# Two copies to the upper partitions: transfers issued by GpSimd in place of ScalarE calls, in a convolution and GELU kernel on one core

## The chip, the cores and the metric

The kernel runs on one core of a Trainium2 chip. The metric is the device time of one execution in microseconds; the time before is the median of three runs. Engines are named as the profile names them: PE (TensorE), with its weight loads as PEld, DVE (VectorE), ACT (ScalarE), POOL (GpSimd) and SP, which only issues transfers.

## The reference

A causal depthwise convolution of seven taps, its weights softmaxed for each of eight heads, feeds a two-layer network with an exact GELU and no biases. Cut to what matters:

```python
# x: (8, 4096, 192), weight: (8, 7), moe_w_in: (192, 2048), moe_w_out: (2048, 192), all float32
w = softmax(weight, axis=-1)                       # one set of 7 taps for each head of 24 channels
conv[b, s, h, g] = sum_k w[h, k] * x_pad[b, s + k, h, g]     # 6 rows of zeros ahead of each sequence
h = conv.reshape(32768, 192) @ moe_w_in
out = (0.5 * h * (1 + erf(h / sqrt(2)))) @ moe_w_out
```

## The kernel before, in words

**Blocks.** The 32768 rows are two halves of 16384. A block takes the same stretch of both halves, one on partitions 0 to 63 (LO), the other on 64 to 127 (UP). There are 35 blocks: six of 256 rows a half, then 29 of 512. For each block DVE transposes the input (`t`, line 968) and computes the taps (calls 1 to 6, lines 338 and 343; the last writes `xc`). The first tap (`f`, line 1107) is computed by ACT; in blocks 13, 18, 23 and 28 two thirds of it are left to DVE as call `0`. PE multiplies by `w_in` (line 1242) in 16 slices into two PSUM buffers `hp`, ACT applies the GELU to each slice (line 1149) into `gT`, and PE multiplies by `w_out` in the next block's time, interleaved with that block's first product. A slice's product has to wait until the GELU two slices earlier has emptied its buffer.

**Two forms of the second product.** In N blocks it is computed directly (line 1327): 48 rounds of four 64x64 matmuls side by side, beside 48 of the first product. The 17 blocks of the list `ST` are S blocks (9, 10, 12, 14, 15, 17, 19, 20, 22, 24, 25, 27, 29 to 33). There a Strassen-like scheme (line 1376) saves PE four rounds, 92 in place of 96 in the block that follows, at the cost of sums on other engines. Ahead of the products DVE, or POOL by accumulating transfers, forms sums of parts of `gT`: `S1`, `S3`, `Dn`, `S4` (lines 662 to 699; `cp` is the plain copy of 512 KB, line 673, ahead of an accumulated `Dn`). Behind them partial products in four PSUM banks X, D, Y and V are joined:

- ACT (`st_copy`, line 740): `p15` copies X to an SBUF tile `gs`; `e` copies a piece of V into D; `p3` copies X's upper half to `tqs`; `u` copies X's lower half to `uu[LO]`. Then `-g` writes -U to `gs[UP]`, and `-u` writes -U to `uu[UP]`, both read from `uu[LO]`.
- DVE (`st_post`): `k0` (line 746) takes `gs` from Y's upper half, `k4` (line 754) adds Y to `gs`, `k3` (line 750) adds `uu` to `tqs`. Then `ev.0`, `ev.1`, `ev.2` (lines 461 and 766) transpose the results into `osb`, from which SP stores them.

`gs` and `tqs` have two buffers each, `uu` one. A bank that a block gives back is taken by a later one: `k4` frees Y, and if the next block is an S block too it takes that bank as its V. PE writes V some 8 us after the start of the block in which that product runs.

**The order** of the work is written out. `LIST` gives DVE's order by block (it runs ahead of PE by up to a block), `SLOT` says before which of a block's 16 GELUs ACT does what (`2:u.9` in list 11: `u` of block 9 ahead of GELU 2 of block 11), and `GLIST` is the order of POOL's queue: transfers, and the six columns that a block's convolution takes over from the block before (`halo`). Every engine works its queue strictly in order, so an instruction that waits holds all behind it. In the text below S + 8 means 8 us after the first `w_in` matmul of the block in which PE is.

Of the kernel before, what the change touches and what calls it, by code (L numbers as in the profile page):

```python
# [11 lines left out]
def bass_lightweight_conv__then__act_gelu_exact_kernel(  # L12
# [63 lines left out]
        9: "t10 ev.0.6 ev.2.6 1 ev.1.6 2 3 4 5 6",  # L76
        10: "t11 ev.0.7 1 2 3 4 ev.1.7 ev.2.7 5 6",
        11: "t12 1 2 3 S1.0.9 4 5 S1.1.9 ev.0.8 ev.1.8 S1.2.9 6",
        12: "Dn.1.9 ev.2.8 S3.2.9 1 S4.0.9 2 S4.1.9 k0.0.9 3 S1.0.10 4 5 S1.1.10 ev.2.9 t13 S1.2.10 Dn.0.10 6",
        13: "S3.2.10 k4.0.9 Dn.1.10 S4.0.10 S4.1.10 t14 k0.0.10 0 ev.0.9 1 2 ev.2.10 k3.0.9 3 ev.1.9 4 5 6",  # L80
        14: "t15 1 2 3 S1.0.12 ev.0.11 4 5 k4.0.10 k3.0.10 S1.1.12 S1.2.12 ev.1.11 ev.1.10 Dn.1.12 ev.2.11 S3.2.12 6",
        15: "S4.0.12 t16 S4.1.12 ev.0.10 k0.0.12 1 2 3 ev.2.12 4 5 6",
        16: "1 t17 2 3 S1.0.14 k3.0.12 4 ev.1.12 ev.0.13 k4.0.12 5 S1.1.14 ev.0.12 ev.2.13 S1.2.14 ev.1.13 Dn.1.14 6",
        17: "S3.2.14 S4.0.14 t18 S4.1.14 1 k0.0.14 S1.0.15 2 3 4 S1.1.15 ev.2.14 Dn.0.15 S1.2.15 5 S3.2.15 6",
        18: "k4.0.14 S4.0.15 Dn.1.15 S4.1.15 k0.0.15 0 ev.0.14 1 2 3 k3.0.14 ev.1.14 ev.2.15 t19 4 5 k4.0.15 6",
        19: "t20 ev.0.15 S1.0.17 1 2 ev.0.16 3 k3.0.15 S1.1.17 4 S1.2.17 ev.1.16 S3.2.17 5 ev.2.16 S4.0.17 Dn.1.17 S4.1.17 ev.1.15 6",
        20: "k0.0.17 t21 1 2 3 ev.2.17 4 5 6",
# [12 lines left out]
        33: "k0.0.30 t34 1 2 S1.0.31 k3.0.29 S1.1.31 Dn.0.31 ev.2.30 ev.1.29 S1.2.31 S4.0.31 3 S3.2.31 4 k4.0.30 ev.0.29 Dn.1.31 S4.1.31 k0.0.31 5 6",  # L100
        34: "k3.0.30 S1.0.32 1 ev.2.31 ev.1.30 Dn.0.32 S1.1.32 S1.2.32 S3.2.32 2 3 k4.0.31 ev.0.30 S4.0.32 Dn.1.32 S4.1.32 ev.0.31 k0.0.32 4 5 S1.0.33 6",
        35: "ev.2.32 S1.1.33 S1.2.33 k3.0.31 S3.2.33 ev.1.31 Dn.0.33 Dn.1.33 k4.0.32 ev.0.32 S4.0.33 k0.0.33 S4.1.33 k3.0.32 ev.1.32 ev.2.33 k4.0.33 ev.0.33 k3.0.33 ev.1.33",
# [3 lines left out]
        8: "0:f0.10 4:f1.10 6:f2.10",  # L106
        9: "1:f0.11 2:f1.11 5:f2.11 8:f0.12 8:f1.12",
        10: "0:f2.12 7:p15.9 13:e.9",
        11: "0:p3.9 2:u.9 4:-g.9 6:p15.10 8:f2.13 10:f0.14 11:-u.9 13:e.10 15:f1.14",
        12: "1:p3.10 2:u.10 4:f2.14 5:-g.10 8:-u.10 11:f0.15 13:f1.15",  # L110
        13: "0:f2.15 7:p15.12 10:f0.16 11:f1.16 13:e.12",
        14: "0:f2.16 2:u.12 3:-g.12 4:p3.12 8:-u.12 9:f0.17 10:f1.17",
        15: "5:f2.17 7:p15.14 8:f2.18 13:e.14",
        16: "0:p3.14 2:u.14 4:-g.14 6:p15.15 11:-u.14 13:e.15",
        17: "0:u.15 2:p3.15 4:-g.15 5:f0.19 6:f1.19 8:f2.19 11:f0.20 12:-u.15",
        18: "4:f1.20 7:p15.17 8:f2.20 11:f0.21 13:e.17 15:f1.21",
        19: "1:p3.17 3:f2.21 4:u.17 7:-g.17 8:f0.22 9:-u.17 12:f1.22",
        20: "0:f2.22 7:p15.19 12:f2.23 13:e.19",
        21: "0:p3.19 2:u.19 4:-g.19 6:p15.20 9:-u.19 13:e.20",
        22: "1:p3.20 2:u.20 4:f0.24 5:-g.20 6:f1.24 8:f2.24 9:-u.20 12:f0.25",  # L120
        23: "5:f1.25 7:p15.22 9:f2.25 11:f0.26 13:e.22",
        24: "0:f1.26 2:p3.22 3:u.22 4:f2.26 7:-g.22 8:f0.27 9:f1.27 11:-u.22 12:f2.27",
        25: "6:p15.24 13:e.24",
        26: "0:p3.24 2:u.24 4:-g.24 6:p15.25 8:-u.24 10:f2.28 12:f0.29 13:e.25",
        27: "1:p3.25 2:u.25 3:-g.25 5:f1.29 6:f2.29 9:f0.30 12:-u.25",
        28: "2:f1.30 4:f2.30 7:p15.27 10:f0.31 10:f1.31 13:e.27",
        29: "0:p3.27 2:f2.31 4:u.27 7:-g.27 9:-u.27 12:f0.32",
        30: "0:f1.32 2:f2.32 7:p15.29 9:f0.33 10:f1.33 12:f2.33 14:e.29",
        31: "0:p3.29 2:u.29 4:-g.29 6:p15.30 8:-u.29 10:f0.34 10:f1.34 13:f2.34 14:e.30",
# [60 lines left out]
    with es:  # L190
# [27 lines left out]
        tq = sbt("tq", [128, TB], F32)  # L218
        hp = [pst("hp%d" % i, [128, 2 * TB]) for i in range(2)]
# [37 lines left out]
        S_UH = sem("S_UH")  # L257
        S_ST = sem("S_ST")
# [3 lines left out]
        S_AD = {k: sem("S_AD" + k) for k in ("S3.0", "S3.1", "S3.2", "Dn.0", "Dn.1", "cp.0", "cp.1")}  # L262
# [447 lines left out]
        def st_copy(a, m, name):  # L710
# [6 lines left out]
            if name[0] != "-":  # L717
                st_done(a, m, {"p15": max("P1", "P5", key=FORM[m][1].get), "e": "Ea", "p3": "P3", "u": "P6"}[name])
            if name == "e":
                dst, src = bank(BK[m]["D"], UP, HA), bank(BK[m]["V"], LO, HA)  # L720
            else:
                dst, src = {
                    "p15": (gs(m)[:, :], bank(BK[m]["X"])),
                    "u": (uu[LO, :], xb(LO)),
                    "-u": (uu[UP, :], uu[LO, :]),
                    "p3": (tqs(m)[LO, :], xb(UP)),
                    "-g": (gs(m)[UP, :], uu[LO, :]),
                }[name]
            if name[0] == "-":
                a.wait_ge(S_AC, ac(m, "u"))  # L730
# [3 lines left out]
            if name == "-g":  # L734
                a.wait_ge(S_DP, dp(m, "k0"))
# [4 lines left out]
            a.activation(out=dst, in_=src, func=AF.Copy, scale=-1.0 if name[0] == "-" else 1.0).then_inc(S_AC)  # L740

        def st_post(v, m, name):
            if name == "k0":
                st_done(v, m, "P7")
                v.wait_ge(S_AC, ac(m, "p15"))
                ins = v.tensor_tensor(tqs(m)[UP, :], bank(BK[m]["Y"], UP), gs(m)[UP, :], ALU.subtract)
            elif name == "k3":
                v.wait_ge(S_AC, max(ac(m, "-u"), ac(m, "p3")))
                v.wait_ge(S_DP, dp(m, "k0"))
                ins = v.tensor_tensor(tqs(m)[:, :], tqs(m)[:, :], uu[:, :], ALU.add)  # L750
            else:
                v.wait_ge(S_MM2, MMC[m + 1])
                v.wait_ge(S_AC, ac(m, "-g"))
                ins = v.tensor_tensor(gs(m)[:, :], bank(BK[m]["Y"]), gs(m)[:, :], ALU.add)
# [25 lines left out]
        def store(e, m):  # L780
# [714 lines left out]
```

## Time and profile before

| | |
|---|---|
| median of 3 runs | 667.44 us (666.6 to 667.59) |
| profiled execution | 668.08 us, of which the span from first to last instruction is 666.1 us |
| granted TensorE clock | 1.000 |
| busy, share of the span | PE 99%, PEld 68%, DVE 92%, ACT 91%, POOL 13% |
| GELU calls, line 1149 | 510 of 1.023 us |
| `-u`, line 740, uu from uu | 17 of 0.629 us |
| `-g`, line 740, gsm or p5s from uu | 17 of 0.63 us |
| `u`, line 740, uu from ob | 17 of 0.582 us |
| first taps of 512 columns, line 1107 | 73 of 0.718 us |
| tap of 1536 elements, line 343 | 145 of 1.807 us |
| `k0`, `k4`, `k3` | 0.695, 0.68 and 0.68 us |

A row of the profile names line, engine, operation and what is written from what; buffer numbers are left out. A `busy` PE is not a PE at its peak, since matmuls are pipelined and their ends are modelled; so the prediction reads PE's progress from the times at which its blocks start. "Idle before" is an engine's idle time just ahead of an instruction, with what ended it.

### The profile page before, as it was taken

Reading aid. Unit: us, or ns where it says so; the run is one execution under the profiler, and the core shown is the slowest. Engines: PE = TensorE matmul, PEld = TensorE weight load, DVE = VectorE, ACT = ScalarE, POOL = GpSimd, SP = SyncE. Lnnn points to the kernel's source line nnn. Section 1 sums busy time; section 2 is a strip of 40 time slices with the busy share of each in tenths; the row PEclk is TensorE's granted clock in tenths of the full one; section 3 lists DMA queues with packets and bytes.
Section 4 is the critical chain, followed back from the end, with each engine's and each line's share of the span. In section 5 each row is a group of like instructions: output and inputs, shape, how many; then the busy total and the mean of one; then the engine's idle time right before and its main releaser. Section 6 shows DMA issues by size and latency. Waiting matters only on the chain.

```text
span 666.1 us, 27899 instructions
## 1 busy us (share of the span) xinstructions
PE 660.9 (99%) x12776; PEld 450.1 (68%) x12776; DVE 615.3 (92%) x550; ACT 608.7 (91%) x723; POOL 86.1 (13%) x137
## 2 busy tenths in 40 slices
PE   8999999999999999999999999999999999999998
PEld 8999655557755657655757665756665766777678
DVE  5889998999999989999999999999999999999962
ACT  8899988888999998999998999998999999999994
POOL 8000540020002020002020101010101010111000
PEclk9999999999999999999999999999999999999999
DMA  9745674566044859144849145849245558223345
GB/s 154 158 99 135 108 122 97 101 146 140 18 116 94 186 125 218 19 96 113 190 101 224 31 96 123 182 97 208 51 96 113 143 121 185 50 50 81 76 95 136
DMA packets 144422, 78.14 MB, mean 117 GB/s; under 512 B 129329, under 2 KB 137585, under 8 KB 144305
## 3 DMA queue, kind: packets, MB, share of 16 engines
q1 hardware_dynamic: 129328, 49.42, 33.2%
q0 software_dynamic: 13856, 26.36, 20.0%
q8 instruction: 100, 1.64, 1.1%
q10 hardware_dynamic: 1120, 0.59, 0.3%
q14 instruction: 18, 0.14, 0.1%
HBM read 31.51 MB, written 25.17 MB: 85 GB/s over the span
## 4 chain that ended last, share of the span: by engine, by line
PE 96%; DMA 2%; DVE 1%; POOL 1%; issue 0%; ACT 0%; DVEq 0%; POOLq 0%
PE hp L1242 49%; PE ob L1376 24%; PE ob L1327 17%; PE ob L1282 4%; DMA xin<-in_x_dram 1%; PE ob L1432 1%; PE hp L1432 1%; DVE acc L343 1%; DMA win<-in_moe_w_in_dram 1%; POOL win L825 0%; DVE xT L968 0%; POOL xTb L358 0%; DVE xc L343 0%; DVE acc L338 0%; POOL wout L857 0%
## 5 line engine op out<-in xcount | busy, mean ns | idle before, releaser
L1149 ACT ACTIVATE gT<-hp 128x1024 bf16<-128x1024 f32 x510 | 512.0, 1023 | 45.6 <-PE hp L1242 39.2
L1242 PE MATMUL hp<-xc,win 64*64 64x512 bf16 (+2 forms) x6036 | 426.3, 366 | 0.7 <-DVE xc L343 0.5
L343 DVE SCALAR_TENSOR_TENSOR acc<-xT,wcol,acc 128x1536 f32<-128x1536 f32 (+1 forms) x165 | 282.3, 1711 | 7.3 <-ACT acc L1107 4.1
L1242 PEld LDWEIGHTS hp<-xc,win 64*64 64x64 bf16 (+1 forms) x6036 | 212.4, 105 | 105.7 <-ACT gT L1149 13.4
L1376 PE MATMUL ob<-gT,wot 64*64 64x512 bf16 x1088 | 206.5, 376 | 0.0
L1376 PE MATMUL ob<-gT,wst 64*64 64x512 bf16 (+2 forms) x1088 | 191.2, 323 | 0.0
L1327 PE MATMUL ob<-gT,wot 64*64 64x512 bf16 x2112 | 144.8, 376 | 0.0
L1376 PE MATMUL ob<-s_S,wot 64*64 64x384 bf16 (+2 forms) x816 | 125.6, 305 | 0.0
L1376 PEld LDWEIGHTS ob<-gT,wst 64*64 64x64 bf16 x1088 | 93.3, 107 | 13.7
L1327 PEld LDWEIGHTS ob<-gT,wot 64*64 64x64 bf16 x2112 | 64.4, 107 | 49.6
L1376 PEld LDWEIGHTS ob<-gT,wot 64*64 64x64 bf16 x1088 | 83.2, 107 | 18.4 <-DVE osb L766 0.5
L1376 PE MATMUL ob<-s_S,wst 64*64 64x512 bf16 x272 | 75.1, 376 | 0.0
L1376 PE MATMUL ob<-s_Dn,wst 64*64 64x512 bf16 x272 | 75.0, 376 | 0.0
L1376 PEld LDWEIGHTS ob<-s_S,wot 64*64 64x64 bf16 x816 | 64.3, 107 | 15.3
L968 DVE STREAM_TRANSPOSE xT<-xin 128x1536 f32<-128x1536 f32 (+2 forms) x39 | 59.3, 1530 | 4.6 <-DMA xin<-in_x_dram 3.7
L343 DVE SCALAR_TENSOR_TENSOR xc<-xT,wcol,acc 128x1536 bf16<-128x1536 f32 (+1 forms) x33 | 56.6, 1716 | 1.1 <-PE hp L1242 0.5
L662 POOL DMA_DIRECT2D gT<-gT x34 | 29.5, 866 | 211.0 <-DVE s_S L690 211.0
L1107 ACT ACTIVATE acc<-xT,wcol 128x512 f32<-128x512 f32 (+1 forms) x79 | 55.1, 701 | 0.0
L690 DVE TENSOR_TENSOR s_S<-gT 128x1024 bf16<-128x1024 bf16 (+1 forms) x51 | 43.5, 855 | 3.0 <-ACT gT L1149 2.8
L1282 PE MATMUL ob<-wout,gT 64*128 64x192 bf16 x768 | 42.1, 243 | 0.5 <-issue 0.5
L699 DVE TENSOR_TENSOR s_S<-gT,s_Dn 128x2048 bf16<-128x2048 bf16 x34 | 40.9, 1211 | 0.7
L1282 PEld LDWEIGHTS ob<-wout,gT 64*128 64x128 bf16 x768 | 35.1, 94 | 4.0 <-issue 0.7
(90 smaller groups left out, 388.1 us busy)
## 6 DMA issues: line engine op xcount, KB each, us to landing
out_dram<-osb SPq DMA_DIRECT2D x124, 192.0 KB, 3.6
xin<-in_x_dram SPq DMA_DIRECT2D x116, 192.0 KB, 4.2
gT<-gT POOLq DMA_DIRECT2D x17, 512.0 KB, 5.0
s_Dn<-gT POOLq DMA_DIRECT2D x9, 512.0 KB, 2.9
s_Dn<-s_S POOLq DMA_DIRECT2D x9, 512.0 KB, 6.5
gT<-gT POOLq DMA_DIRECT2D x17, 256.0 KB, 3.8
xin<-in_x_dram SPq DMA_DIRECT2D x18, 96.0 KB, 2.7
win<-in_moe_w_in_dram POOLq DMA_DIRECT2D x24, 64.0 KB, 3.5
```

Of the source, the lines that this page charges most:

```text
L343: return e.scalar_tensor_tensor(dst, src, wk, a, op0=ALU.mult, op1=ALU.add)
L662: e.dma_start(quad(m, 1, 0, k, k1 - k), quad(m, 0, 0, k, k1 - k), accum_op=ALU.add).then_inc(S_AD["S3.%d" % q], 16)
L690: ins = v.tensor_tensor(t("S1"), quad(m, 1, 0, k, n), quad(m, 1, 1, k, n), ALU.add)
L699: ins = v.tensor_tensor(t("S4"), quad(m, 0, 1, k, n), t("Dn"), ALU.add)
L968: v.transpose(out, src).then_inc(S_TR)
L1107: a.activation(out=acc[n % 2][:, p * TB : p * TB + w], in_=ap(xT[n % 2], p * XW + HX, [[NP * XW, 128], [1, w]]), func=AF.Copy, scale=wcol[ ...
L1149: a.activation(out=ap(gT[n % 2], (i % 2 * NF + i // 2) * TB if n in ST else i * c * 2 * w, dst), in_=ap(ob, 2 * TB, [[4 * TB, 128], *src[1 ...
L1242: ins = t.matmul(hbuf(u, slice(fo, fo + fw), o, w), ap(win, f1, [[NP * F, 64], [2, fw]]), xc[n % 2][r, p * TB : p * TB + w], start=(p == 0 ...
L1282: ins = t.matmul(bb[sub], gT[m % 2][r, c0 : c0 + 128], wout[r, CH[sub][i] * C : (CH[sub][i] + 1) * C], start=(ph == 0 and k == 0), stop=(p ...
L1327: ins = t.matmul(bank(BK[m][j], slice(64 * h, 64 * h + 64), w), ap(wot, 64 * hf * NF * C + CH[h][i] * C + 64 * j, [[NF * C, 64], [1, 64]]) ...
L1376: ins = t.matmul(bank(BK[m][bk], slice(64 * cg, 64 * cg + 64))[:, c0 : c0 + w], wt_, x, start=(e == mine[0]), stop=(e == mine[-1] or e in ...
L1432: ins = t.matmul(banks(m, g)[h], gT[m % 2][:, c0 : c0 + 128], wout[:, CH[h][i] * C : (CH[h][i] + 1) * C], start=(i == 0), stop=(i == NF - 1),)
```

## The change

`-g` and `-u` are no ScalarE calls any more. POOL issues two transfers in their place, `cg` (`uu[LO]` to `gs[UP]`) and `cu` (`uu[LO]` to `uu[UP]`), 64 rows of 512 float32 each. A transfer can't negate, so the signs go elsewhere: `p15` copies X with scale -1, `k0` adds, `k4` subtracts, and `k3` multiplies `uu` by a column `sgn` (1 on the lower, -1 on the upper partitions, set by two memsets on DVE at the start) before it adds. `k4` waits for `cg`, `k3` for `cu`, `cg` for `u` and `k0`, and the next S block's `u` for the `cg` before it. `LIST`, `SLOT` and `GLIST` are new for blocks 8 to 35; they hold the same calls but for the replaced ones, in another order. The parts of the lists that the prediction speaks of are kept here.

```diff
 LIST
-        12: "Dn.1.9 ev.2.8 S3.2.9 1 S4.0.9 2 S4.1.9 k0.0.9 3 S1.0.10 4 5 S1.1.10 ev.2.9 t13 S1.2.10 Dn.0.10 6",
-        18: "k4.0.14 S4.0.15 Dn.1.15 S4.1.15 k0.0.15 0 ev.0.14 1 2 3 k3.0.14 ev.1.14 ev.2.15 t19 4 5 k4.0.15 6",
-        20: "k0.0.17 t21 1 2 3 ev.2.17 4 5 6",
-        34: "k3.0.30 S1.0.32 1 ev.2.31 ev.1.30 Dn.0.32 S1.1.32 S1.2.32 S3.2.32 2 3 k4.0.31 ev.0.30 S4.0.32 Dn.1.32 S4.1.32 ev.0.31 k0.0.32 4 5 S1.0.33 6",
+        12: "ev.1.8 S1.2.9 S3.2.9 ev.2.8 1 Dn.1.9 t13 S4.0.9 k0.0.9 S4.1.9 S1.0.10 2 3 4 ev.2.9 5 S1.1.10 S1.2.10 Dn.0.10 S3.2.10 Dn.1.10 6",
+        18: "0 k4.0.14 Dn.1.15 S4.0.15 k3.0.14 S4.1.15 k0.0.15 1 t19 ev.1.14 2 ev.0.14 ev.2.15 3 4 5 6",
+        20: "ev.0.15 S4.0.17 k0.0.17 S4.1.17 1 t21 2 3 ev.2.17 4 5 6",
+        34: "ev.0.30 S1.0.32 S1.1.32 1 k3.0.30 ev.2.31 Dn.0.32 S1.2.32 S3.2.32 2 3 k4.0.31 S4.0.32 Dn.1.32 S4.1.32 ev.1.30 k0.0.32 4 5 S1.0.33 S1.1.33 6",
-        35: "ev.2.32 S1.1.33 S1.2.33 k3.0.31 S3.2.33 ev.1.31 Dn.0.33 Dn.1.33 k4.0.32 ...
+        35: "ev.2.32 k3.0.31 S1.2.33 S3.2.33 Dn.0.33 ev.0.31 k4.0.32 ev.1.31 Dn.1.33 ...
...
 SLOT
-        16: "0:p3.14 2:u.14 4:-g.14 6:p15.15 11:-u.14 13:e.15",
-        30: "0:f1.32 2:f2.32 7:p15.29 9:f0.33 10:f1.33 12:f2.33 14:e.29",
-        34: "0:p3.32 2:u.32 4:-g.32 6:p15.33 10:-u.32 14:e.33",
-        35: "0:u.33 0:-g.33 0:-u.33 0:p3.33",
+        16: "0:p3.14 2:u.14 6:p15.15 13:e.15 14:f0.19",
+        30: "0:f0.32 2:f1.32 5:f2.32 6:p15.29 8:f0.33 9:f1.33 12:f2.33 14:e.29",
+        34: "0:p3.32 2:u.32 6:p15.33 13:e.33 15:u.33",
+        35: "0:p3.33",
...
 st_dma, on POOL
+            if name in ("cu", "cg"):
+                e.wait_ge(S_AC, ac(m, "u"))
+                if name == "cg":
+                    e.wait_ge(S_DP, dp(m, "k0"))
+                dst = uu if name == "cu" else gs(m)
+                e.dma_start(dst[UP, :], uu[LO, :]).then_inc(S_AD[name], 16)
+                return
...
 st_copy, on ACT
-                    "-u": (uu[UP, :], uu[LO, :]),
-                    "-g": (gs(m)[UP, :], uu[LO, :]),
-            if name[0] == "-":
-                a.wait_ge(S_AC, ac(m, "u"))
-            if name == "-g":
-                a.wait_ge(S_DP, dp(m, "k0"))
             if name == "u" and i:
                 a.wait_ge(S_DP, dp(ST[i - 1], "k3"))
-            a.activation(out=dst, in_=src, func=AF.Copy, scale=-1.0 if name[0] == "-" else 1.0).then_inc(S_AC)
+                a.wait_ge(S_AD["cg"], 16 * i)
+            a.activation(out=dst, in_=src, func=AF.Copy, scale=-1.0 if name == "p15" else 1.0).then_inc(S_AC)
...
 st_post, on DVE: k0, k3, k4
-                ins = v.tensor_tensor(tqs(m)[UP, :], bank(BK[m]["Y"], UP), gs(m)[UP, :], ALU.subtract)
+                if ST.index(m) > 1:
+                    v.wait_ge(S_EV, EV[ST[ST.index(m) - 2], 1])
+                ins = v.tensor_tensor(tqs(m)[UP, :], bank(BK[m]["Y"], UP), gs(m)[UP, :], ALU.add)
-                v.wait_ge(S_AC, max(ac(m, "-u"), ac(m, "p3")))
+                v.wait_ge(S_AD["cu"], 16 * ST.index(m) + 16)
+                v.wait_ge(S_AC, ac(m, "p3"))
...
-                ins = v.tensor_tensor(tqs(m)[:, :], tqs(m)[:, :], uu[:, :], ALU.add)
+                ins = v.scalar_tensor_tensor(
+                    tqs(m)[:, :], uu[:, :], sgn[:, 0:1], tqs(m)[:, :], op0=ALU.mult, op1=ALU.add
+                )
-                v.wait_ge(S_AC, ac(m, "-g"))
-                ins = v.tensor_tensor(gs(m)[:, :], bank(BK[m]["Y"]), gs(m)[:, :], ALU.add)
+                v.wait_ge(S_AD["cg"], 16 * ST.index(m) + 16)
+                ins = v.tensor_tensor(gs(m)[:, :], bank(BK[m]["Y"]), gs(m)[:, :], ALU.subtract)
...
 GLIST, on POOL (from the new one)
+            "S3.1.12 Dn.0.12 cu.0.12 cg.0.12 halo.16 cp.0.14 S3.0.14 halo.17 Dn.0.14 "
+            "S3.1.14 S3.0.15 S3.1.15 cg.0.14 halo.18 cu.0.14 halo.19 cu.0.15 cg.0.15 "
...
+            "cu.0.30 halo.34 S3.0.32 S3.1.32 cg.0.31 cu.0.31 S3.0.33 S3.1.33 cg.0.32 "
+            "cu.0.32 cg.0.33 cu.0.33 "
```

## The prediction

> **What bounds the kernel now.** I read the busy shares, then the chain of waits, then who waits for whom between 146.56 and 653 us, then timelines of PE, ACT and DVE.
>
> ```profile
> PE 660.9 (99%) x12776; PEld 450.1 (68%) x12776; DVE 615.3 (92%) x550; ACT 608.7 (91%) x723; POOL 86.1 (13%) x137
> ...
> PE 96%; DMA 2%; DVE 1%; POOL 1%; issue 0%; ACT 0%; DVEq 0%; POOLq 0%
> ```
> ```profile
> PEld hp L1242 <- ACT gT L1149: 12.9, 47, 0.5
> ...
> DVE p5s L754 <- ACT p5s L740: 2.3, 4, 0.8
> ...
> DVE gsm L754 <- ACT gsm L740: 1.6, 2, 0.9
> ...
> PEld ob L1376 <- DVE osb L766: 0.5, 1, 0.5
> ```
>
> The chain is TensorE's. What matters is how far its blocks are from their shortest length. In PE's timeline the first L1242 matmul of blocks 15, 16 and 17 starts at:
>
> ```profile
> 248.00 0.39 PE L1242 MATMUL hp<-xc,win 64*64 64x512 bf16 x4
> ```
> ```profile
> 267.86 0.38 PE L1242 MATMUL hp<-xc,win 64*64 64x512 bf16 x1
> ...
> 287.90 0.38 PE L1242 MATMUL hp<-xc,win 64*64 64x512 bf16 x3
> ```
>
> Block 15 takes 19.87 us (to the rounding), block 16 20.04. I read all starts from block 10 (146.56) to block 34 (632.80). A block whose predecessor is in ST (92 rounds of four matmuls) never takes less than 19.87, and eight take just that; one after an N block (96 rounds) never under 20.72. So a round is 0.216 us, and the 16 + 8 blocks cost at least 16 x 19.87 + 8 x 20.72 = 483.7. They take 632.80 - 146.56 = 486.2, and block 34 to the first L1432 matmul (653.00) 20.20 instead of 19.87. **All stalls of the steady part are 2.5 + 0.3 us**: most is weight loads waiting for a GELU, 0.29 is block 32's start, waiting for ev.2.30 (the L766 line). More than 2.8 can't be won there. Why GELUs are late, in block 16, on ACT:
>
> ```profile
> 268.72 0.59 ACT L740 ACTIVATE wtf<-ob 64x512 f32<-64x512 f32 x1
> 269.34 1.94 ACT L1149 ACTIVATE gT<-hp 128x1024 bf16<-128x1024 f32 x2
> 271.16 0.58 ACT L740 ACTIVATE uu<-ob 64x512 f32<-64x512 f32 x1
> 271.64 1.93 ACT L1149 ACTIVATE gT<-hp 128x1024 bf16<-128x1024 f32 x2
> 273.59 0.63 ACT L740 ACTIVATE p5s<-uu 64x512 f32<-64x512 f32 x1
> 274.25 1.94 ACT L1149 ACTIVATE gT<-hp 128x1024 bf16<-128x1024 f32 x2
> 276.07 0.61 ACT L740 ACTIVATE gsm<-ob 128x512 f32<-128x512 f32 x1
> 276.55 1.04 ACT L1149 ACTIVATE gT<-hp 128x1024 bf16<-128x1024 f32 x1
> ```
>
> In order: p3, GELUs 1-2, u, 3-4, -g, 5-6, p15, 7. Two GELUs and u take 271.64 - 269.34 = 2.30; two GELUs and -g take 274.25 - 271.64 = 2.61, though u and -g last about the same: -g overlaps neither neighbour. A GELU by itself is 0.92 (271.16 - 269.34, halved), so -g costs 2.61 - 1.84 = 0.77 of the queue. From p3 to GELU 7, 276.55 - 268.72 = 7.83 us hold six GELUs, when PE gives six slices in 6 x 1.242 = 7.45.
>
> **The change, part by part.** *34 ScalarE calls go* (17 -g, 17 -u): 34 x 0.77 = 26 us of ACT's queue. First taps (f) stay 70, so no work comes in their place. Without -g the stretch above is 7.06, under 7.45: that stall is gone. It is the same in blocks 11, 21, 26, 31, 33 and 34. The densest new stretch is block 30, with five f (0.59 of queue each) and a p15 (0.46) in slots 0 to 9: 10 x 0.92 + 3.4 = 12.6 against 12.4. In block 16 an excess of 7.83 - 7.45 = 0.38 cost PE 0.17, so the two hp buffers ride out some 0.2: nothing. Saved: 2.5 - 0.29 + 0.16 (block 34) = **-2.4**; bounds -1.0 (only the seven -g stalls) and -2.8.
>
> *34 transfers come* on POOL's queue, 64 rows of 2 KB each (128 KB). cg gates k4, and k4 frees bank Y, which the next S block takes as V. Eight pairs S,S are tight (m = 9, 14, 19, 24, 29 to 32). For m = 14:
>
> ```profile
> 274.32 0.69 DVE L754 TENSOR_TENSOR p5s<-ob,p5s 128x512 f32<-128x512 f32 x1 [0.33 <-ACT p5s L740]
> ```
> ```profile
> 275.99 0.33 PE L1376 MATMUL ob<-gT,wst 64*64 64x128 bf16 x2
> ```
>
> u ends at 271.74, and PE first writes V at 275.99, or 275.85 without the stall. Take off k4 (0.69) and 0.17 for two handovers: cg may take 275.85 - 271.74 - 0.86 = **3.25 us** from issue to landing. No row shows 128 KB on this queue. The nearest is cp, a plain SBUF copy of 512 KB issued by POOL; the least is 2.2 (96 KB stores, other queues).
>
> ```profile
> L673 POOL DMA_DIRECT2D s_Dn<-gT x9: 554/554/915, 141.3 to 543.7; - x9
> ...
> DMA to landing us min/median/max: 2.8/2.9/5.2
> ```
> ```profile
> 271.80:274.30 2.50, 2.50 (x52) 1.50 (x48) 2.19 (x2) 2.45 (x4) 0.11 (x1) 1.00 0.00 0
> ...
> 636.70:639.20 2.50, 2.50 (x52) 1.45 (x48) 1.70 (x2) 2.45 (x4) 0.00 (x0) 1.00 0.78 187
> ```
>
> These are windows of 2.5 us after u of m = 14 and 32; the last columns are DMA share and GB/s. The eight windows after u are idle (share 0.00 to 0.03) but for m = 31 (0.41) and 32 (0.78), and there the new lists move ev.1.30 and ev.1.31, whose stores follow them, behind k4, and S1.1.32 and S1.1.33, which release accumulates, forward. I take 2.5: **0**; bounds 0 and (5.2 - 3.25) x 8 = +15.6. Where DVE comes to k4 first it waits, with taps and sums queued behind: some tenths, as for -g before (3.9 us in six waits), covered by the lead of the taps (9 to 18 us from block 10 to 32). Only block 34 has little: its last tap ends at 632.10, PE starts at 632.80. In list 34 S1.1.33 (0.69) stands in for ev.0.31 (0.70).
>
> On POOL's queue halos stand behind cg and cu, as halo.16 behind cu.12 and cg.12, ready with u.12 near 228.6: two issues of 0.55 to 0.9 put it at 230.4, and the tap that needs it comes at about 231: 0. Accumulates for PE (S3) stand ahead of the cg in question. The next u waits for the cg before it, 16 us or more later.
>
> *cu and k3*: nothing reads k3 soon; cu's landing 1 us behind cg's is covered. k3 becomes a SCALAR_TENSOR_TENSOR: 128x768 takes 1016 ns and 128x1536 1807, so 512 takes 0.75 against 0.68: 17 x 0.07 = 1.2 us of DVE, against 15 us idle in the steady part; about 0.2 before block 34's 0.70: 0, bounds 0 and +0.5.
>
> *k0 between S4.0 and S4.1* (lists 12 and 20). k0 waits for P7, out 10.2 us after the block's start (in DVE's timeline k0.33 waits for PE until 643.10; block 34 starts at 632.80; less a stall of 0.1); with k0 (0.73) and S4.1 (1.2) that is 12.1, and P3's second half starts 56 rounds in, 12.1: **+0.2** for both, bounds 0 and +0.6.
>
> *Signs, memsets, sgn*: p15 with scale -1 and k0, k4 keep their form. The memsets stand ahead of DVE's 1.2 us wait for the weight. If that cover went, 0.2.
>
> *u.33 before the last GELU* (slot 15 of block 34) is a cost:
>
> ```profile
> 652.65 0.38 PE L1376 MATMUL ob<-s_Dn,wst 64*64 64x512 bf16 x1
> ...
> 653.00 2.81 PE L1432 MATMUL ob<-wout,gT 128*128 128x192 bf16 x32
> ```
> ```profile
> 652.67 1.02 ACT L1149 ACTIVATE gT<-hp 128x1024 bf16<-128x1024 f32 x1 [0.27 <-PE hp L1242]
> 653.59 0.58 ACT L740 ACTIVATE uu<-ob 64x512 f32<-64x512 f32 x1
> ```
>
> u waits for P6, whose last matmul (s_Dn) ends at 653.03. The GELU then starts at 653.55 and ends at 654.57, not 653.69. The thirteenth of these matmuls needs it at 653.00 + 12 x 0.083 = 653.99: **+0.6** on the path to the end; bounds +0.3 and +0.9.
>
> Sum: -2.4 + 0.2 + 0.6 = -1.6. The profiled execution took 668.08 (span 666.1 and 2.0 around it), 0.1% above the median; it becomes 666.5, and the median of 667.44 becomes **665.8**. The measurement tells about 0.2% (1.3 us) from no change, so this is just beyond.
>
> **Rivals.** *cg lands too late* (slower): place, the V bank of eight blocks; point, 3.25 us; price, 8 us for each us beyond. For it: a maximum of 5.2, and 3.2 to 6.4 for the accumulates on this queue; against: four times fewer bytes and idle windows. At 4.0: 665.8 + 6.0 = 671.8; at 3.75: 669.8. Chance 0.17.
>
> *The GELU stalls stay* (no change): ACT itself waits 25 us for PE in this part, so most of the freed time falls into waits, and new bursts of f in slots 0 to 6 could stall as the -g did. With half of the 2.4 left: 667.0; with nothing saved, 668.2. Chance 0.30.
>
> *POOL's issue is held by DVE* (slower): held for one tap (1.81), cg would land 4.3 to 4.7 after its issue, eight times 1.05 to 1.45 late: 674 to 677. Against: 34 accumulate issues took 857/862/962 ns (min/median/max) under a DVE busy 97% of that time. Chance 0.06. The Trainium skill (SBUF — State Buffer, "SBUF: two separate sides") says that GpSimd can't write descriptors while VectorE runs in a two-port mode, and tells of a transfer of 620 ns that took 3100; those 34 rows show no such hold.
>
> **How the numbers follow.** The forecast holds 0.47, all of it faster; the second rival is the no-change case (0.30); the others are slower (0.23). The range runs from 664.6 (all of 2.8, no tail cost) to 670.0 (cg at 3.75); outside lie the third rival, a later cg and a little below: 0.18. The forecast's own range is 664.6 to 666.1.
>
> **What would show it.** Right: blocks after S,S pairs at 19.87; weight loads waiting for GELU under 4 us; cg landing in 2.2 to 3.0; L754 waits for a DMA under 0.5 each; 0.6 between L1432's twelfth and thirteenth matmul. Wrong: PE waiting for DVE's L754 at slice 6, cg landings over 3.25, or POOL issues near 2 us.

## The result and the profile after

The changed kernel takes **668.79 us** (median; 667.64 to 669.63), the kernel before, run beside it, 667.14 (666.60 to 668.13). The ratio is **1.0022, 95% interval 1.0014 to 1.0029**: slower by 0.22%, 1.65 us, where 665.8 was forecast. 668.79 lies inside the range given (664.6 to 670.0), but the change was forecast to make the kernel faster and made it slower. The profiled execution took 668.96 with a span of 667.2 (before: 668.08 and 666.1).

The page of the changed kernel, busy times and the chain of waits:

```profile
PE 660.8 (99%) x12776; PEld 483.8 (73%) x12776; DVE 616.0 (92%) x552; ACT 591.0 (89%) x689; POOL 109.2 (16%) x171
...
PE 94%; ACT 2%; DMA 2%; DVE 1%; issue 1%; SPq 0%; DVEq 0%; ACTq 0%
```

ACT is busy 17.7 us less with 34 calls fewer (723 to 689), as meant. PE's work is the same, yet its share of the chain fell by two points: the chain now passes more often through other engines (ACT 2% instead of 0%, issue 1% instead of 0%). Who waits for whom between 146.56 and 653 us (engine, line, waited for: us in total, times, longest):

```profile
PEld hp L1258 <- ACT gT L1165: 4.6, 23, 0.3
...
DVE p5s L764 <- DMA p5s<-uu: 2.5, 2, 1.9
PEld ob L1392 <- DVE osb L776: 1.9, 5, 0.5
PEld ob L1392 <- DVE p5s L764: 1.4, 2, 0.9
...
PEld ob L1392 <- DVE gsm L764: 1.0, 2, 0.8
```

Weight loads wait 4.6 us for a GELU instead of 12.9. In their place stand waits for L764 (that is k4, L754 before) and for L776 (ev.2, L766 before). The starts of the blocks, from PE's timeline:

| us | before | after |
|---|---|---|
| start of block 10 | 146.56 | 145.97 |
| blocks 10 to 33 (floor 483.7) | 486.24 | 487.11 |
| block 34 to the end of the span | 33.30 | 34.12 |

The floor is the one of the prediction, and the spans are read to 0.1 us.

The steady part has 3.4 us of stalls instead of 2.5, and the tail is 0.8 longer. The gaps from slice to slice of the L1258 matmuls show where:

- 0.71 and 0.63 at slice 6 of blocks 11 and 32, where PE first writes V: PE waits for k4.9 and k4.30 (k4 of blocks 9 and 30), and these for their cg.
- 1.0 where DVE comes late to an entry: blocks 26 (0.22, k4.24, its cg long landed), 31 (0.25, ev.2.29, and 0.14 further on), 32 (0.19, ev.2.30) and 33 (0.23, ev.2.31).
- 0.23 at slice 2 of block 31, where PE waits for the accumulate S3.0.30, which lands 3.77 us into the block.
- 0.34 at the end of block 33, where block 34's last tap is late: DVE has waited 0.59 for cg.30 and 0.47 for cg.31 before it.
- some 0.5 in smaller ones.

The GELU stalls did go. Here is ACT's timeline in block 16, where u stands between two pairs of GELUs and -g no longer follows:

```profile
269.25 1.94 ACT L1165 ACTIVATE gT<-hp 128x1024 bf16<-128x1024 f32 x2
271.08 0.58 ACT L743 ACTIVATE uu<-ob 64x512 f32<-64x512 f32 x1
271.56 1.93 ACT L1165 ACTIVATE gT<-hp 128x1024 bf16<-128x1024 f32 x2
273.63 1.02 ACT L1165 ACTIVATE gT<-hp 128x1024 bf16<-128x1024 f32 x1
```

From 271.56 to 273.63 two GELUs take 2.07; before, two GELUs and -g took 2.61. Block 16 takes 19.88 instead of 20.04, block 21 19.87 instead of 20.01.

What came instead, in block 32 (timelines of POOL, DVE and PE):

```profile
596.12 0.56 POOL L666 DMA_DIRECT2D p5s<-uu  x1 [5.00 <-ACT uu L743]
```
```profile
599.98 0.69 DVE L764 TENSOR_TENSOR p5s<-ob,p5s 128x512 f32<-128x512 f32 x1 [0.59 <-DMA p5s<-uu]
```
```profile
600.73 0.35 PE L1392 MATMUL ob<-gT,wst 64*64 64x128 bf16 x2 [0.43 <-DVE p5s L764]
```

cg.30 is issued at 596.12 in 0.56 us and lands 3.77 later; DVE stands idle for it, and PE for DVE. Of all 34 transfers:

```profile
DMA to landing us min/median/max: 2.2/3.0/5.3
```

And the tail, PE's and ACT's timelines (L1448 is L1432 before):

```profile
653.10 1.16 PE L1448 MATMUL ob<-wout,gT 128*128 128x192 bf16 x12
654.79 1.82 PE L1448 MATMUL ob<-wout,gT 128*128 128x192 bf16 x20 [0.53 <-ACT gT L1165]
```
```profile
653.24 0.59 ACT L743 ACTIVATE uu<-ob 64x512 f32<-64x512 f32 x1 [0.72 <-PE ob L1392]
```

The hole stands behind the twelfth matmul, as forecast; from the start of the first group of 32 output matmuls to that of the second it takes 656.45 - 653.10 = 3.35 instead of 2.65.

### The profile page after: what moved, and what is told of

Same layout as the page of the kernel before. It is cut to its first block, busy times and chain, and to the rows that moved or that the text cites. A ratio compares the mean times of both kernels' runs of the same rounds, so it can differ in the third digit from the quotient of the medians.

```text
span 667.2 us, 27902 instructions
## 1 busy us (share of the span) xinstructions
PE 660.8 (99%) x12776; PEld 483.8 (73%) x12776; DVE 616.0 (92%) x552; ACT 591.0 (89%) x689; POOL 109.2 (16%) x171
## 4 chain that ended last, share of the span: by engine, by line
PE 94%; ACT 2%; DMA 2%; DVE 1%; issue 1%; SPq 0%; DVEq 0%; ACTq 0%
PE hp L1258 48%; PE ob L1392 23%; PE ob L1343 17%; PE ob L1298 5%; ACT gT L1165 1%; PE hp L1448 1%; PE ob L1448 1%; DMA p5s<-uu 1%; DMA gsm<-uu 1%; DMA xin<-in_x_dram 1%; PE ob L1201 0%; DVE xc L345 0%; PE ob L1258 0%; DVE s_S L699 0%; ACT uu L743 0%
## 5 line engine op out<-in xcount | busy, mean ns | idle before, releaser
L1258 PE MATMUL hp<-xc,win 64*64 64x512 bf16 (+2 forms) x6036 | 436.2, 366 | 0.3 <-DVE xc L345 0.2
L1258 PEld LDWEIGHTS hp<-xc,win 64*64 64x64 bf16 (+1 forms) x6036 | 232.3, 106 | 85.8 <-ACT gT L1165 5.0
L1392 PE MATMUL ob<-gT,wot 64*64 64x512 bf16 x1088 | 208.1, 376 | 0.0
L1343 PE MATMUL ob<-gT,wot 64*64 64x512 bf16 x2112 | 148.0, 376 | 0.0
L1392 PE MATMUL ob<-s_S,wot 64*64 64x128 bf16 (+2 forms) x816 | 126.1, 305 | 0.0
L1343 PEld LDWEIGHTS ob<-gT,wot 64*64 64x64 bf16 x2112 | 74.1, 107 | 39.9 <-DVE osb L776 0.3
L1392 PEld LDWEIGHTS ob<-gT,wot 64*64 64x64 bf16 x1088 | 83.7, 107 | 10.6 <-DVE osb L776 1.9
L1298 PEld LDWEIGHTS ob<-wout,gT 64*128 64x128 bf16 x768 | 33.3, 94 | 4.8
```

The costliest lines, as they stand in the source:

```text
L1258: ins = t.matmul(hbuf(u, slice(fo, fo + fw), o, w), ap(win, f1, [[NP * F, 64], [2, fw]]), xc[n % 2][r, p * TB : p * TB + w], start=(p == 0 ...
L1298: ins = t.matmul(bb[sub], gT[m % 2][r, c0 : c0 + 128], wout[r, CH[sub][i] * C : (CH[sub][i] + 1) * C], start=(ph == 0 and k == 0), stop=(p ...
L1343: ins = t.matmul(bank(BK[m][j], slice(64 * h, 64 * h + 64), w), ap(wot, 64 * hf * NF * C + CH[h][i] * C + 64 * j, [[NF * C, 64], [1, 64]]) ...
L1392: ins = t.matmul(bank(BK[m][bk], slice(64 * cg, 64 * cg + 64))[:, c0 : c0 + w], wt_, x, start=(e == mine[0]), stop=(e == mine[-1] or e in ...
```

## The experiments

The medians of the kernel before beside these runs were 667.08 to 667.18. The last three columns are from one profiled execution each. The start of block 10, which carries the head, differs from profile to profile by up to 2.7 us among kernels whose head is the same (145.2 to 147.9), so stages are compared, and totals only by medians (the profile of late_lists is of its longest execution, 670.25). The granted clock was 1.000 in all but old_both (0.997). The end of a profile scatters too: from the start of the last group of output matmuls to the end of the span it took 5.2 us before, 5.5 in the changed kernel, and 5.7, 6.1 and 6.2 in fetch_20, late_lists and fetch_64, where that group starts at most 0.02 us off the changed kernel's, counted from the start of block 34.

| kernel | median us | ratio to before, 95% | start of 10 | 10 to 33 | 34 to end |
|---|---|---|---|---|---|
| tail | 669.72 | 1.0035 (1.0023 to 1.0047) | 145.48 | 486.17 | 35.35 |
| old_both | 678.73 | 1.0180 (1.0163 to 1.0198) | 145.20 | 495.13 | 36.07 |
| old_cg | 670.73 | 1.0044 (1.0032 to 1.0056) | 145.84 | 486.85 | 36.21 |
| old_cu | 676.33 | 1.0139 (1.0125 to 1.0153) | 146.14 | 493.83 | 33.83 |
| fetch_20 | 671.28 | 1.0067 (1.0054 to 1.0080) | 145.60 | 488.58 | 34.32 |
| fetch_64 | 668.11 | 1.0012 (1.0004 to 1.0021) | 146.82 | 485.11 | 34.87 |
| tail_act | 666.94 | 0.9995 (0.9985 to 1.0005) | 145.54 | 486.83 | 33.13 |
| late_lists | 667.75 | 1.0011 (1.0002 to 1.0020) | 147.91 | 485.88 | 34.70 |
| combo | 667.28 | 1.0003 (0.9995 to 1.0012) | 146.50 | 485.44 | 33.65 |
| old_lists | 668.74 | 1.0026 (1.0016 to 1.0036) | 145.40 | 487.13 | 34.27 |
| before_shift | 668.23 | 1.0016 (1.0007 to 1.0024) | 146.80 | 486.17 | 33.33 |
| mended | 667.87 | 1.0012 (1.0003 to 1.0020) | 146.62 | 487.56 | 33.12 |
| mended_later | 667.68 | 1.0010 (1.0001 to 1.0018) | 146.07 | 486.26 | 33.47 |
| final | 666.21 | 0.9982 (0.9974 to 0.9991) | 146.35 | 484.53 | 33.22 |
| final48 | 665.86 | 0.9979 (0.9970 to 0.9987) | 145.24 | 485.75 | 33.12 |

**tail.** Only u.33 is put back behind the last GELU.

```
-        34: "0:p3.32 2:u.32 6:p15.33 13:e.33 15:u.33",
-        35: "0:p3.33",
+        34: "0:p3.32 2:u.32 6:p15.33 13:e.33",
+        35: "0:u.33 0:p3.33",
```

> The changed kernel with u.33 put back behind block 34's last GELU (slot 35), nothing else. Theory A (u.33 ahead of the GELU delays the last output matmuls): the 0.53 us hole between matmuls 12 and 13 of L1448 goes, the time falls by 0.4 to 0.6 us from 668.8 to about 668.3, and block 34 to the end takes 33.4 to 33.6 us instead of 34.12. Rival (the last sums wait for u.33, k4.33 and k3.33 at the very end, so moving u.33 back only moves the wait): no change, 668.8.

669.72: no gain, and the rival holds. The 0.53 hole is gone, and another stands ahead of the third group of output matmuls (a group is 32 of them):

```profile
657.78 2.80 PE L1448 MATMUL ob<-wout,gT 128*128 128x192 bf16 x32 [0.67 <-DVE gsm L764]
```

That group writes bank Y, which k4.33 frees, and k4.33 waited 7.1 us for cg.33 (issued 653.14, landed 656.74). So u.33 stands ahead of the GELU to give cg.33 time: the tail is a ninth tight place, which the prediction did not list. Of the 1.2 us that this stage is longer than the changed kernel's, only 0.1 lies ahead of the last group; the rest lies behind its start (6.6 us instead of 5.5) and stays open.

**old_cg, old_cu, old_both.** The lists of the kernel before without its -g and -u, and one of the transfers or both put in at their places in time; the copy that is no transfer stays a ScalarE call.

```
 GLIST (old_both)  ... S3.1.15 cg.0.14 halo.19 cu.0.14 cg.0.15 cp.0.17 S3.0.17 Dn.0.17 cu.0.15 S3.1.17 ...
```

> As old_both, but only cg is a transfer; the copy to the upper half of uu stays a ScalarE call at its old place. Theory A: the seven -g stalls go (1.0 us or more) and cg, with no cu behind it, lands 2.2 to 2.6 us after its issue wherever no accumulate is still moving: 665.0 to 666.1. Theory B: cg late as before, 667 or more.

> As old_both, but only cu is a transfer; the copy to the upper half of gs stays a ScalarE call at its old place. Theory A: the -g stalls stay, of the 2.3 us of GELU stalls at most 1.2 goes: 666.0 to 667.1. Theory B (transfers on POOL's queue cost through contention with accumulates): 667.2 to 668.

> The three lists of the kernel before, with -g and -u taken from ScalarE's slots and cg and cu put into POOL's list at the places in time where -g and -u stood; the rest as in the changed kernel. Theory A (the transfers win the GELU stalls, 2.3 us, and the loss is in the newly found lists and u.33): 664.9 to 665.9, weight loads waiting for GELU under 5 us in the steady part, blocks 31 to 33 without the stalls at slices 0 that the changed kernel shows. Theory B (the transfers themselves cost, since cg lands late whatever the lists): 667 or more, with PE waiting for L764 at slice 6 in several S,S pairs.

All three are slower than theory A, old_cu than both. In old_cg cg does land late near the end (3.55, 3.73 and 3.94 us for m = 30, 31 and 32), so theory B's sign is right there, though not whatever the lists (below). What they show well is the GELU part. In the kernel before, blocks 11, 16, 21, 26, 31 and 33 each lose 0.12 us at slice 5, where -g delayed the GELUs. With -g gone none of this is left in old_cg and old_both; in old_cu, with -g kept, 0.08 to 0.13 stays in all of them but block 16. (The lengths of blocks 16, 21 and 26 are 19.91, 19.88 and 19.87 in old_cg, 20.01, 20.08 and 20.18 in old_cu, and 20.04, 20.01 and 20.02 before; in old_both they are 20.05, 19.97 and 20.01, since PE waits at their start for other entries.) The large losses of old_cu and old_both come from where I put cu: behind accumulates. In old_cu, cu.15 was issued at 302.77, right behind Dn.0.17, and landed at 309.14, 0.3 after it: 6.37 us. DVE waited at k3 with S1 queued behind, and PE for S1 (the waits of old_cu's steady part):

```profile
DVE tq L760 <- DMA uu<-uu: 7.0, 2, 3.8
PEld ob L1393 <- DVE s_S L699: 6.8, 5, 2.9
```

old_both shows the same wait at k3 (7.2 us in two). So a copy that has slack still has to be issued ahead of the accumulates, as the new POOL list does with cu.15.

**old_lists.** As tail_act (below), but with before's lists and cu right behind cg.

```
-            "... halo.20 S3.0.17 S3.1.17 cp.0.17 Dn.0.17 cu.0.17 halo.21 halo.22 cg.0.17 ..."
+            "... cp.0.17 S3.0.17 Dn.0.17 S3.1.17 halo.20 halo.21 cg.0.17 cu.0.17 cp.0.19 S3.0.19 ..."
```

> tail_act (copies of m = 33 by ScalarE) with the three lists of the kernel before: -g and -u out of ScalarE's slots, cg and cu side by side in POOL's list right behind the end of u and k0. Against tail_act only the lists differ. Theory L (the lists had to be found anew: k4 stands in the old lists where -g ended 0.63 us after its start, the transfer takes 2.2 or more, and VectorE then waits with taps and sums queued behind): stalls of 0.3 to 1.0 in blocks 31 to 34, total 668 to 670. Rival (the lists do not matter): 666.9.

668.74, theory L: against tail_act's 666.94 the old lists cost 1.8 us. The stalls at slice 6 are 0.67 in block 32, 0.42 in 33 and 1.01 in 34, where DVE waited 2.41 at k4.32. The copies waited for had landed 3.81 (cg.30), 3.95 (cg.31) and 3.87 us (cg.32) after their issue. So the old lists lose with these transfers, but how much of it is the order and how much the late landings (the first two met a packet of the kind described under fetch_20) isn't separated; tail_act loses 0.71 in block 32 to cg.30 too.

**tail_act.** m = 33 keeps the two ScalarE copies.

```
+        35: "0:u.33 0:-g.33 0:-u.33 0:p3.33",
+                if m == ST[-1]:
+                    v.wait_ge(S_AC, ac(m, "-g"))
```

> The changed kernel with the two copies of the last block of ST, m = 33, made by ScalarE as before (u, -g, -u, p3 behind the last GELU, plain copies with the changed kernel's signs), and no transfer for that block. Theory A (u.33 stands ahead of the last GELU only to give cg.33 time to land before L1448's third group needs bank Y): from block 34's first matmul to the end 33.3 us as before instead of 34.1, total 668.0. Rival (the tail's loss has another cause): 668.8.

Block 34 to the end: 33.13, as theory A says. The total is 1.85 us below the changed kernel's median, more than the 1.0 of the stage; what the rest is was not settled.

**late_lists.** Six entries moved in VectorE's lists.

```
-  27: "... S3.2.25 t28 6"                    28: "k4.0.24 0 ..."
+  27: "... S3.2.25 6"                        28: "k4.0.24 t28 0 ..."
-  32: "... 2 3 S1.0.30 4 Dn.0.30 ev.2.29"    33: "... Dn.0.31 ev.2.30"
+  32: "... 2 S1.0.30 3 4 ev.2.29 Dn.0.30"    33: "... ev.2.30 Dn.0.31"
-  34: "... k3.0.30 ev.2.31 ... S1.0.33 S1.1.33 6"   35: "ev.2.32 k3.0.31"
+  34: "... ev.2.31 k3.0.30 ... S1.0.33 6"           35: "ev.2.32 S1.1.33 k3.0.31"
```

> The changed kernel with VectorE's lists of blocks 27, 28 and 32 to 35 mended where the trace shows TensorE waiting for a late entry: t28 behind k4.24, S1.0.30 one tap earlier, ev.2.29, ev.2.30 and ev.2.31 one entry earlier, S1.1.33 behind the last tap of block 34. Theory L (the newly found lists put entries that free a bank or feed an accumulate behind others): the waits of blocks 26 (0.22), 31 (0.25 and 0.23), 32 (0.19) and 33 (0.23 and 0.34) go, 1.0 to 1.4 us less, total about 667.6. Rival (VectorE is simply full there and each swap only moves the wait): 668.8 within 0.3.

667.75; the steady part is 1.23 us shorter, and blocks 31 and 33 are at 19.87. That is theory L, but in block 26 the rival was right: the wait for k4.24 went, and 0.3 us came back at slices 8 and 13, since S4.0.25 now stood behind t28.

**fetch_20 and fetch_64.** Why does cg take 2.2 us in one block and 3.8 in the next? The DMA view of the changed kernel, 596.1 to 600 us, has cg.30, cu.30 and one packet more (queue, kind: packets, MB, share of 16 engines):

```profile
q0 software_dynamic: 96, 0.26, 29.2%
q8 instruction: 1, 0.02, 2.2%
...
p5s<-uu POOLq DMA_DIRECT2D x1, 128.0 KB, 3.8
```

The trace holds 100 such packets of 16 KB, one per 257 instructions of TensorE on average (25711 matmuls, weight loads and entries of its sequencer). That is 64 bytes an instruction, so I take them for TensorE's instructions being fetched; each packet takes 0.9 to 2.0 us. The trace does not name the DMA engine, but it counts a landing in 16 steps: of cg.30's, fifteen have come by 2.23 us after the issue and the last comes at 3.77; of cg.14's, with no packet near, all sixteen come from 2.00 to 2.18. So one of sixteen engines is late. The accumulate S3.0.30, named above, is the same case: fifteen steps by 4.38 us, the last at 6.34, 1.1 after the end of a packet. In these two kernels other warm-up matmuls (the ones at TensorE's start that compute nothing that is used) shift the packets against the work.

```
-            for i in range(48):
-                t.matmul(hp[1][:, 0:128], one, one)
+            few = nc.const_aps.tensor(1.0, (128, 55), BF16)
+            for i in range(112):
+                t.matmul(hp[1][:, 0:55], one, few)
```

> The changed kernel; the 48 warm-up matmuls of 128 columns at TensorE's start become 68 of 90 columns, so 40 more instructions (a weight load and a matmul each) run ahead of the rest and TensorE's later instruction fetches (16 KB packets on the queue named instruction, one for about 257 TensorE instructions, some 6 us apart) come about 0.95 us earlier against the work. Theory F (a cg lands late where such a packet, 0.9 to 1.35 us on one DMA engine, is under way when the copy's data moves, 1.0 to 2.1 us after the issue; it then lands about 1.25 after the packet's end): cg.9 2.9, cg.30 2.8, cg.31 and cg.27 2.2 instead of 3.74, 3.77, 3.06 and 3.09, cg.19 and cg.29 about 3.1 instead of 2.2; the stalls of blocks 11 and 32 at slice 6 (0.71 and 0.63) go, total about 667.4. Theory Q (late because cu stands right behind cg, or because of accumulates ahead of it on POOL's queue): cg.9 and cg.30 stay at 3.5 to 3.8, total 668.8.

> As fetch_20 with 112 warm-up matmuls of 55 columns: 128 more instructions, half a period, fetches about 3 us earlier against the work. Theory F: cg.9, cg.30, cg.31, cg.27, cg.19 and cg.29 all land 2.2 to 2.5 after issue; cg.14 and cg.24 have a packet starting 1.7 to 2.0 after their issue and may be late (up to 3.9, then a stall of 0.6 in block 16 or 26). Total about 667.5. Theory Q: as the changed kernel, 668.8.

fetch_64: cg.9, 19, 24, 29, 30, 31 and 32 land at 2.17 to 2.41, and cg.14, one of the two named as at risk, at 3.05, which costs 0.12 in block 16. Block 32's 0.63 is gone, block 11's 0.71 is 0.19, block 31's 0.23 and the 0.34 at the end of block 33 are gone too, and the steady part falls by 2.0 us. Theory F's total, about 667.5, is missed by 0.6. In the same place as above there is no packet:

```profile
q0 software_dynamic: 97, 0.26, 39.0%
...
p5s<-uu POOLq DMA_DIRECT2D x1, 128.0 KB, 2.2
```

fetch_20 bears out the landings (cg.30 2.73, cg.31 2.18, cg.27 2.20, cg.19 3.03, cg.29 3.20; only cg.9, 3.42, had been expected sooner), but not the total: the packets now meet accumulates. S3.1.10 lands 4.62 after its issue instead of 3.40 (again fifteen steps by 3.24), and in block 11 PE waits for it (in block 18 another 1.0 us goes where PE waits for S4, which follows Dn.0.17, whose last step comes 1.5 us behind the fifteenth):

```profile
PEld ob L1393 <- DMA gT<-gT: 1.5, 1, 1.5
```

Over the changed kernel and the ten kernels here that keep its lists or mend them (88 copies at the eight tight places): the 61 with no such packet under way from 1.0 to 1.7 us after the issue landed at 2.17 to 2.43; the 27 that met one landed at 2.35 to 3.85, 26 of them 1.1 to 1.5 us after the packet's end; of each of the 27, fifteen steps had come by 2.18 to 2.52. Theory F holds for the landings, and Q falls: in fetch_64 cu stands as close behind cg as before. A second cause shows with the old lists: cg.32 lands at 3.94 in old_cg and at 3.87 in old_lists with fifteen steps as late as 3.36 and 3.54, and there the DMA share from issue to landing is 0.89 (0.40 in the changed kernel, where it lands at 2.19).

The Trainium skill (DMA: Bandwidth & Descriptors, "Why a DMA increments its semaphore by 16 and not by 1") says that a DMA runs on up to 16 engines, which finish independently, and that only the full count of 16 means that all data has landed. The runs agree: fifteen steps by 2.23 us and the sixteenth at 3.77 make a copy of 3.77.

**before_shift.** The same 112 warm-up matmuls in the kernel before.

> The kernel before with the 112 warm-up matmuls of 55 columns alone. Theory F (the fetches matter only where a transfer is near the path; the kernel before has none there but the accumulates): 667.1 within 0.4. Rival (the shift of the fetches or the other warm-up is itself a gain or a loss, whatever the copies): more than 0.6 away from 667.1, and then the gain of fetch_64 and of combo is not the transfers'.

The rival, for the total: 668.23, 1.1 us slower. But the steady part is 486.17 (486.24 before) and the tail 33.33 (33.30), so the loss should lie ahead of block 10. The two profiles don't show it there: block 10 starts only 0.24 later, as the profile of the kernel before is itself of an execution 0.9 above its median. So the stage gain of fetch_64 is the transfers'; of its 2.0 us only 0.7 is in the median. Its tail is 0.75 longer in its profile, all of it behind the start of the last group, and 112 warm-up matmuls cost 1.1 in before_shift. What in the head costs that stays open.

**combo.** tail_act, late_lists (with S4.0.25 ahead of t28, S1.1.10 ahead of tap 5) and 112 warm-up matmuls.

> The changed kernel with the three mends together: 112 warm-up matmuls of 55 columns (as fetch_64), the copies of m = 33 by ScalarE (as tail_act), VectorE's lists mended as in late_lists but with S4.0.25 kept ahead of t28 and the tap 0, and S1.1.10 ahead of tap 5 in list 12. If the three losses are separate and add up: blocks 10 to 33 take 484.2 to 484.6 us (floor 483.7), block 34 to the end 33.1 to 33.3, total 665.3 to 666.2, below the kernel before. Rival (what one mend wins another gives back, the mended lists shifting issues into packets or accumulates): 666.9, no better than tail_act.

667.28: the rival. cg.14 met a packet again (3.66), 0.74 in block 16; the head may cost what it costs in before_shift, but one profile can't show that.

**mended and mended_later.** These are combo with the old warm-up, or with 21 matmuls of 293 columns, and three more list moves, of which one is shown.

```
-  12: "... ev.2.9 S1.1.10 5 S1.2.10 ... Dn.1.10 6"            13: "k4.0.9 S4.0.10 ..."
+  12: "... ev.2.9 S1.1.10 5 S1.2.10 ... Dn.1.10 k4.0.9 6"     13: "S4.0.10 ..."
```

> combo without the other warm-up (48 matmuls of 128 columns again), with VectorE's lists mended further: ev.2.25 ahead of tap 2 in list 28, k4.9 ahead of tap 6 in list 12, k4.30 ahead of ev.1.29 in list 33; copies of m = 33 by ScalarE. Theory: the head costs nothing extra, cg.9 and cg.30 still meet an instruction packet (3.6 to 3.8) and cost about 0.5 each, the other list waits are gone: blocks 10 to 33 take 484.9 to 485.4 us, block 34 to the end 33.1 to 33.4, total 665.9 to 666.4, below the kernel before. Rival (the gains of single mends do not survive together, as combo's did not): 667.

> mended with 21 warm-up matmuls of 293 columns, so 54 instructions fewer ahead of the rest and the instruction packets about 1.3 us later against the work. Theory F: the packets that met cg.9 and cg.30 (starting 1.4 and 1.1 us after the issue) start after their data, and both land at 2.2 to 2.4; cg.19 and cg.29 (none within) keep 2.2 to 2.5, cg.31 may meet one late in its data. Blocks 10 to 33 take 484.0 to 484.7 us. Total 665.2 to 665.9 if the head keeps its length, about 666.5 if it pays 1 us as with 112 matmuls. Rival (the packets are not what delays): blocks 10 to 33 as in mended.

The packets came out much as expected (mended: cg.9 at 3.71 and cg.30 at 3.31; mended_later: all eight copies at 2.18 to 2.92, blocks 11 and 32 without their stalls), the totals did not: one of my moves was wrong. With k4.9 ahead of tap 6, DVE waited there for cg, t15 came late, and the GELUs behind its first tap (ACT's timeline):

```profile
195.75 0.72 ACT L1134 ACTIVATE acc<-xT,wcol 128x512 f32<-128x512 f32 x1 [1.04 <-DVE xT L995]
```

Block 12 took 21.74 instead of 20.72. A second loss, 0.9 in block 23, was S3.0.22, queued behind Dn.0.22 and halo.25.

**final and final48.** k4.9 back behind tap 6, halo.25 and S3.0.22 ahead of Dn.0.22; final with 21 warm-up matmuls, final48 with 48.

```
-   ... cg.0.20 cp.0.22 Dn.0.22 halo.25 S3.0.22 S3.1.22 ...
+   ... cg.0.20 halo.25 cp.0.22 S3.0.22 Dn.0.22 S3.1.22 ...
```

> mended_later with k4.9 back behind tap 6 (ahead of it, it made VectorE's t15 and so a first tap and the GELUs of block 12 1.0 us late) and with halo.25 and S3.0.22 ahead of Dn.0.22 in POOL's list (S3.0.22 landed 0.9 us too late for block 23). Theory F with the lists: blocks 10 to 33 484.3 to 484.9 us instead of 486.26, block 34 to the end 33.1 to 33.5, total 665.4 to 666.2, below the kernel before by 1 us or more. Rival (VectorE, 97 per cent busy, is the next bound, so a stall taken from one block comes back in the next): 667.0 or more.

> final with the 48 warm-up matmuls of 128 columns, so that the instruction packets stand against the copies as in the changed kernel. Theory F: cg.9 and cg.30 land at 3.3 to 3.8 again and cost 0.3 to 0.8 each at slice 6 of blocks 11 and 32; blocks 10 to 33 about 485.3, total 666.2 to 666.8. Rival (the packets do not matter): the same as final.

Both are faster than the kernel before, if by less than 0.3%, and than the changed one: 666.21 (0.9982, 0.9974 to 0.9991) and 665.86 (0.9979, 0.9970 to 0.9987). final's steady part is 484.53, 0.85 above the floor. Of its waits between blocks 10 and 34, one for k4 is left:

```profile
PEld hp L1270 <- ACT gT L1176: 6.0, 31, 0.3
...
PEld ob L1404 <- DVE gsm L774: 0.5, 1, 0.5
```

final48's is 485.75: cg.9 met a packet (3.64, 0.72 in block 11), cg.30 was issued 1.9 us ahead of one and landed at 2.43, where 3.3 to 3.8 was expected. Another 0.5 is lost in block 32, where PE waits for the accumulate S3.0.31: fifteen steps by 4.48 us, the last at 5.97 (5.19 in final). The 1.2 us between the two kernels in the steady part do not show in the totals: final48 is below the 666.2 to 666.8 expected for it and faster than final by 0.35. final's head is 1.1 longer in its profile (146.35 against 145.24).

## Why the prediction was wrong, point by point

- **-2.4, the GELU stalls: right.** Blocks 16 and 21 are at the shortest length (19.88 and 19.87), slice 5 in old_cg and old_cu ties it to -g, and the rival that the stalls stay falls. Block 34 up to the first L1448 matmul gained 0.18 (20.02 instead of 20.20), forecast 0.16. The 4.6 us of weight loads waiting for a GELU are a little over the 4 I had set, and cost PE nothing that the slice gaps show.
- **0 for cg: the failed step.** The allowance of 3.25 us was right: cg.31 at 3.06 cost nothing at slice 6 of block 33, cg.30 at 3.77 cost 0.63 (0.52 by the price) and cg.9 at 3.74 0.71. The value, 2.5, came from windows of DMA share that looked idle (0.00 to 0.03). One of these windows of the kernel before, the one for m = 30:

```profile
596.60:599.10 2.50, 2.50 (x55) 1.37 (x51) 2.50 (x3) 2.45 (x4) 0.00 (x0) 1.00 0.02 7
```

Its 0.02 and 7 GB/s are not idleness: 16 KB in 2.5 us is 6.6 GB/s, and the trace has one such packet there, of 0.93 us. Of the six windows called idle, four show 0.02 or 0.03 and hold one packet each. A quiet copy is even faster than 2.5, 2.2, but a share averaged over 16 engines hides one packet on one engine, and the landing is that of the last engine. Two of eight met one late enough: **+1.34**. Packets also delayed S3.0.30 (0.23), for which the sum had no term, and by way of DVE's waits for cg.30 and cg.31 the last tap of block 34 (0.34; fetch_64 has neither these waits nor this loss). The rival "cg too late" was the right mechanism with its point; I gave it 0.17 and no reason why some would be late and others not. Sharing the price over all eight made its total, 671.8, too high.
- **0 for the waits of DVE and the new lists: the other failed step.** "Covered by the lead of the taps" looked only at taps. The entries that free a bank (ev.2, k4) or feed an accumulate (S1) have no such lead: DVE is busy 97% there, and a list that moves them by one entry shows in PE. This is the **+1.0** of late entries. late_lists, which moves six entries, won 1.23 of the steady part back, the 0.23 and the 0.34 of the packets among them, since an earlier S1 or a later one can cure these as well. The sum held nothing for this; the bounds of cg's term covered it only by chance.
- **+0.6 for u.33: the size right (0.70), the reason missed.** It stands there for cg.33 (tail, tail_act). The prediction counted the tail's cost but not that the last copies are better not transfers at all; with ScalarE's copies the stage takes 33.13.
- **+0.2 for k0 between S4.0 and S4.1: hardly seen.** k0.9 and k0.17 start 10.17 and 10.22 us into blocks 10 and 18, as forecast; block 10 takes 19.87, its floor, and block 18 19.93. **0 for k3: right** (708 to 750 ns against 0.75). **Halos: right**; DVE waits for POOL's copies twice, 0.2 us each, in blocks 19 and 22, which are within 0.04 of their floor.
- **POOL's issue held by DVE: not seen**, 0.52 to 1.07 us, 0.56 in the median, under a DVE busy 97%. No run here shows the hold of which the Trainium skill (SBUF — State Buffer, "SBUF: two separate sides") tells; whether an instruction of DVE here runs in the mode it speaks of, no row says.

In one line: -2.3 GELU and -0.3 the old wait for ev.2.30; +1.3 packets on cg, +0.6 what packets did by way of S3.0.30 and of DVE's waits, +1.0 late list entries, +0.5 smaller stalls; in the tail -0.2 block 34, +0.7 the first output group, +0.3 behind the start of the last. That is +1.6 to +1.7 between the two profiles from block 10 on. The medians differ by 1.65 too, but this agreement is partly luck: the two spans differ by only 1.1, since the head of the profile after is 0.6 shorter, and heads scatter by more than that.

## What to carry to other kernels

Here a copy moved from an engine to a DMA queue traded a fixed 0.6 to 0.8 us of the engine (0.63 its duration, 0.77 with the overlap that it prevented) for a landing that scattered between 2.2 and 3.8 us at the tight places, and up to 5.3 elsewhere. Such a copy may gate the path only where there is room for the upper end. Take that scatter from the packets of all queues, instruction packets included, not from a mean DMA share. And when the engine that consumes the copy is nearly always busy (here 97%), price each entry that its list moves, and keep the copy on the engine where nothing else waits for that engine, as at the end.

## What the runs showed of the hardware that was not expected

- TensorE's instructions are fetched while it runs: 16 KB in one packet, 100 of them in 667 us, one about every 6.5 us, each taking 0.9 to 2.0 us. A copy that meets one has fifteen of its sixteen steps on time and the last late. Here that moves a 128 KB copy from 2.2 to as much as 3.85 us and an accumulate from 3.40 to 4.62.
- Because the packets follow the count of instructions, 40 instructions added at the start moved them by 0.7 to 1.6 us, 1.0 in the mean, against five of the copies, 170 to 620 us later (cg.9, 19, 29, 30 and 31, fetch_20).
- A 128 KB copy issued right behind a 512 KB accumulate on POOL's queue landed 0.3 us after it, 6.4 us after its own issue.
